# A Fourier mixing layer and its channel mix: sequence split 24x128 to 48x64, feature butterfly, paired planes, mirrored half by exchanged weight rows, squares on DVE alone

## Chip, cores and metric

One Trainium2 chip, one core. The metric is the device time of one execution in microseconds. The kernel before has three measured runs: 703.01, 699.72 and 702.3 us, median 702.3.

## The reference, cut to what matters

```python
def reference(x, mu_k, mu_r, w_k, w_v, w_r):      # x: 8 x 3072 x 256
    y = np.fft.fft(np.fft.fft(x, axis=1), axis=2).real
    y_prev = np.concatenate([zeros(8, 1, 256), y[:, :-1, :]], axis=1)
    xk = mu_k * y + (1 - mu_k) * y_prev
    xr = mu_r * y + (1 - mu_r) * y_prev
    k = np.maximum(xk @ w_k, 0)                    # 256 -> 1024
    v = (k * k) @ w_v                              # 1024 -> 256
    r = 1 / (1 + np.exp(-(xr @ w_r)))
    return r * v                                   # 8 x 3072 x 256, f32
```

The input of the channel mix is real, so the half of the spectrum past row 1536 is that of the mirrored row with the feature index mirrored as well: y[S-k, v] = y[k, (256-v) mod 256].

## The kernel before

Each of the 8 batches goes through two parts. The **Fourier part** writes the sequence index as n1 x 128 with n1 = 24. Stage A (`stage_a_group`, L240) multiplies 64 blocks of the loaded `xh` (96 partitions) by a 104-wide table and gives `a_sb`; ACT and DVE take turns at moving its PSUM tile to SBUF (L250, L252). Stage D (`dc_d_step`, L297 to L304) is the Fourier transform over the 256 features: for each of 13 values of k1 two or four matmuls of 512 columns into `psG`, which DVE casts to `g_sb` (L307). Stage C (`dc_c_step`, L313, L316) is the remaining transform over 128, in four 128-wide matmuls, moved by ACT (L319). `refl_step` (L329 to L335) makes the 11 mirrored slabs of y with four matmuls each by two reflection matrices, moved by ACT (L337).

The **channel mix** works in 6 chunks of 512 sequence positions. `mix_block` (L266 to L269) forms xk and xr on DVE. `moe_kmm` runs 8 feature groups per chunk: two 512-wide matmuls into `psK` (L388, L391), a Relu on ACT over 512 columns (L394), and a square (L397) on POOL for even and on DVE for odd groups. `moe_vr` runs, for each of four blocks of 128 positions, eight 256-wide matmuls with w_v (L407) and two with w_r (L412) into one PSUM tile; ACT takes the Sigmoid (L416), DVE multiplies (L418) and SP stores 128 KB (L420).

`stage_moe` sets the order: the kmm block of a chunk (16 matmuls), then two or three `dc_steps` of the next batch with stage A groups of the batch after it, then the vr block of the chunk before. Loads of x are issued by POOL (L221), between its squares. PSUM has six one-bank buffers for everything but `psKV`, which has two. The tables (wd, cm, sm) are made in a prologue on DVE and ACT.

Of the kernel before, what the change touches and what calls it, by code (L numbers as in the profile page):

```python
# [23 lines left out]

@with_exitstack
def kernel(
# [10 lines left out]
    nc = tc.nc  # L39
# [27 lines left out]
    nc.vector.tensor_scalar(out=pcol_f, in0=pcol_i, scalar1=1.0, scalar2=None,
                            op0=ALU.mult)

    col256_i = gen.tile([P, 256], INT32)  # L70
    nc.gpsimd.iota(col256_i, pattern=[[1, 256]], base=0, channel_multiplier=0)
    col128_i = gen.tile([P, 128], INT32)
    nc.gpsimd.iota(col128_i, pattern=[[1, 128]], base=0, channel_multiplier=0)
    col24_i = gen.tile([P, 24], INT32)
    nc.gpsimd.iota(col24_i, pattern=[[1, 24]], base=0, channel_multiplier=0)

    def gen_trig(dst_cos, dst_sin, p_vals, col_i, scale, ncols, pn,
                 sin_scale=1.0, dst_nsin=None):
        u = gen.tile([P, 256], FP32, name="gen_u")[:pn, :ncols]
        r = gen.tile([P, 256], FP32, name="gen_r")[:pn, :ncols]  # L80
        ci = col_i[:pn, :ncols]
        nc.vector.tensor_scalar(out=u, in0=ci, scalar1=p_vals, scalar2=scale,
                                op0=ALU.mult, op1=ALU.mult)
        nc.vector.tensor_scalar(out=r, in0=u, scalar1=MAGIC, scalar2=MAGIC,
                                op0=ALU.add, op1=ALU.subtract)
        nc.vector.tensor_tensor(out=u, in0=u, in1=r, op=ALU.subtract)
        if dst_sin is not None:
            nc.scalar.activation(out=dst_sin, in_=u, func=AF.Sin,
                                 bias=0.0, scale=TWO_PI * sin_scale)
        if dst_nsin is not None:  # L90
            nc.scalar.activation(out=dst_nsin, in_=u, func=AF.Sin,
                                 bias=0.0, scale=-TWO_PI)
        nc.vector.tensor_scalar(out=u, in0=ci, scalar1=p_vals, scalar2=scale,
                                op0=ALU.mult, op1=ALU.mult)
        nc.vector.tensor_scalar(out=u, in0=u, scalar1=0.25, scalar2=None,
                                op0=ALU.add)
        nc.vector.tensor_scalar(out=r, in0=u, scalar1=MAGIC, scalar2=MAGIC,  # L97
                                op0=ALU.add, op1=ALU.subtract)
        nc.vector.tensor_tensor(out=u, in0=u, in1=r, op=ALU.subtract)
        nc.scalar.activation(out=dst_cos, in_=u, func=AF.Sin, bias=0.0,  # L100
                             scale=TWO_PI)

    NKH = 13
    w24_mov = const.tile([96, 4, NKH, 2], FP16)
    nc.vector.memset(w24_mov, 0.0)
    w24_blk = gen.tile([24, NKH, 2], FP16)
    col13_i = gen.tile([P, NKH], INT32)
    nc.gpsimd.iota(col13_i, pattern=[[1, NKH]], base=0, channel_multiplier=0)
    gen_trig(dst_cos=w24_blk[:, :, 0], dst_sin=w24_blk[:, :, 1],
             p_vals=pcol_f[:24], col_i=col13_i, scale=1.0 / N1, ncols=NKH, pn=24,  # L110
             sin_scale=-1.0)
    for g in range(4):
        nc.sync.dma_start(out=w24_mov[24 * g:24 * g + 24, g], in_=w24_blk[:, :, :])
    refl_corner = const.tile([P, 128], FP16)
    refl_anti = const.tile([P, 128], FP16)
    nc.gpsimd.memset(refl_corner, 0.0)
    nc.gpsimd.affine_select(out=refl_corner, in_=refl_corner,
                            compare_op=ALU.not_equal, fill=1.0, base=0,
                            pattern=[[1, 128]], channel_multiplier=1)
    nc.gpsimd.memset(refl_anti, 0.0)  # L120
    nc.gpsimd.affine_select(out=refl_anti, in_=refl_anti,
                            compare_op=ALU.not_equal, fill=1.0, base=-128,
                            pattern=[[1, 128]], channel_multiplier=1)

    wd_r = [const.tile([P, 512], FP16, name=f"wd_r{da}") for da in range(2)]
    wd_i = [const.tile([P, 512], FP16, name=f"wd_i{da}") for da in range(2)]
    dval = gen.tile([P, 1], FP32)
    for da in range(2):
        nc.vector.tensor_scalar(out=dval, in0=pcol_f, scalar1=1.0,
                                scalar2=float(128 * da), op0=ALU.mult, op1=ALU.add)  # L130
        u = gen.tile([P, 256], FP32, name="gen_u")
        r = gen.tile([P, 256], FP32, name="gen_r")
        nc.vector.tensor_scalar(out=u, in0=col256_i, scalar1=dval, scalar2=1.0 / D,
                                op0=ALU.mult, op1=ALU.mult)
        nc.vector.tensor_scalar(out=r, in0=u, scalar1=MAGIC, scalar2=MAGIC,
                                op0=ALU.add, op1=ALU.subtract)
        nc.vector.tensor_tensor(out=u, in0=u, in1=r, op=ALU.subtract)
        nc.scalar.activation(out=wd_i[da][:, 0:256], in_=u, func=AF.Sin,
                             bias=0.0, scale=TWO_PI)
        nc.scalar.activation(out=wd_r[da][:, 256:512], in_=u, func=AF.Sin,  # L140
                             bias=0.0, scale=-TWO_PI)
        nc.vector.tensor_scalar(out=u, in0=u, scalar1=0.25, scalar2=None,
                                op0=ALU.add)
        nc.vector.tensor_scalar(out=r, in0=u, scalar1=MAGIC, scalar2=MAGIC,
                                op0=ALU.add, op1=ALU.subtract)
        nc.vector.tensor_tensor(out=u, in0=u, in1=r, op=ALU.subtract)
        nc.scalar.activation(out=wd_r[da][:, 0:256], in_=u, func=AF.Sin,
                             bias=0.0, scale=TWO_PI)
        nc.scalar.activation(out=wd_i[da][:, 256:512], in_=u, func=AF.Sin,
                             bias=0.0, scale=TWO_PI)  # L150
# [12 lines left out]
    tmp_m = gen.tile([P, 128], FP32)
    for k1 in range(13):
        cb = cosb[:, k1:k1 + 1]
        sb = sinb[:, k1:k1 + 1]
        nsb = nsinb[:, k1:k1 + 1]
        nc.scalar.activation(out=tmp_m, in_=c128, func=AF.Copy, scale=cb)
        nc.vector.scalar_tensor_tensor(out=cm_all[:, k1], in0=s128, scalar=nsb,
                                       in1=tmp_m, op0=ALU.mult, op1=ALU.add)  # L170
        tmp_m2 = gen.tile([P, 128], FP32, name="tmp_m2")
        nc.scalar.activation(out=tmp_m2, in_=s128, func=AF.Copy, scale=cb)
        nc.vector.scalar_tensor_tensor(out=sm_all[:, k1], in0=c128, scalar=sb,
                                       in1=tmp_m2, op0=ALU.mult, op1=ALU.add)
# [10 lines left out]
    def load_weights():  # L185
# [3 lines left out]
        for fc in range(8):  # L189
            nc.gpsimd.dma_start(out=wv_sb[:, fc], in_=wv_dram[fc])  # L190
# [319 lines left out]
```

## Time and profile before

| what | value |
|---|---|
| three runs | 699.72 to 703.01 us, median 702.3 us |
| span of the profiled execution | 697.3 us (its own time is given by this span; the median lies 5.0 us above it) |
| PE busy | 567.6 us, 81% |
| DVE busy | 562.8 us, 81% |
| ACT busy | 380.9 us, 55% |
| POOL busy | 266.0 us, 38% |
| moved by DMA | 39.7 MB, mean 57 GB/s |

Busy shares are averages over the span. Matmuls overlap each other, so PE's busy time counts more than the time between their starts, and the starts tell the rate.

### The profile page before, as it was taken

Reading aid. Unit: us, or ns where it says so; the run is one execution under the profiler, and the core shown is the slowest. Engines: PE = TensorE matmul, PEld = TensorE weight load, DVE = VectorE, ACT = ScalarE, POOL = GpSimd, SP = SyncE. Lnnn points to the kernel's source line nnn. Section 1 sums busy time; section 2 is a strip of 40 time slices with the busy share of each in tenths; the row PEclk is TensorE's granted clock in tenths of the full one; section 3 lists DMA queues with packets and bytes.
Section 4 is the critical chain, followed back from the end, with each engine's and each line's share of the span. In section 5 each row is a group of like instructions: output and inputs, shape, how many; then the busy total and the mean of one; then the engine's idle time right before and its main releaser. Section 6 shows DMA issues by size and latency. Waiting matters only on the chain.

```text
span 697.3 us, 11974 instructions
## 1 busy us (share of the span) xinstructions
PE 567.6 (81%) x4352; PEld 390.1 (56%) x4352; DVE 562.8 (81%) x1036; ACT 380.9 (55%) x955; POOL 266.0 (38%) x281
## 2 busy tenths in 40 slices
PE   0297689887988798887898889989797988988897
PEld 0265366564656556664566546656565645656565
DVE  4569988698797968988887888879889797869764
ACT  3855456545565465554554565565565554555564
POOL 6323333424253243234422353252343253342552
PEclk9999799999999999999999999999999999999999
DMA  6740131042111430032301422111010110111112
GB/s 120 130 91 13 29 83 62 30 106 47 54 39 39 110 65 31 31 86 62 66 31 47 91 48 60 46 45 63 23 39 31 46 47 31 54 39 62 46 60 78
DMA packets 33227, 39.72 MB, mean 57 GB/s; under 512 B 5520, under 2 KB 31376, under 8 KB 31632
## 3 DMA queue, kind: packets, MB, share of 16 engines
q0 software_dynamic: 4800, 13.77, 11.5%
q1 hardware_dynamic: 28368, 25.19, 10.8%
q8 instruction: 34, 0.56, 0.4%
q14 instruction: 25, 0.20, 0.1%
HBM read 27.53 MB, written 25.17 MB: 76 GB/s over the span
## 4 chain that ended last, share of the span: by engine, by line
DVE 54%; PE 23%; ACT 12%; issue 6%; DMA 4%; SPq 0%; ACTq 0%; DVEq 0%
DVE k2t L397 21%; PE psKV L407 12%; ACT k2t L394 9%; DVE xr_sb L267 9%; DVE g_sb L307 6%; DVE xk_sb L269 6%; DVE xk_sb L266 4%; DMA out_dram<-o_sb 3%; DVE o_sb L418 3%; PE psKV L412 3%; DVE a_sb L252 2%; PE psK L388 2%; PE psK L391 2%; PE psY L313 1%; ACT a_sb L250 1%
## 5 line engine op out<-in xcount | busy, mean ns | idle before, releaser
L397 POOL TENSOR_TENSOR k2t<-k2t 128x512 f16<-128x512 f16 x192 | 225.7, 1202 | 392.0 <-ACT k2t L394 391.8
L407 PE MATMUL psKV<-wv_sb,k2t 128*128 128x256 f16 x1536 | 206.5, 277 | 17.9 <-DVE o_sb L418 16.0
L397 DVE TENSOR_TENSOR k2t<-k2t 128x512 f16<-128x512 f16 x192 | 186.5, 999 | 31.3 <-ACT k2t L394 28.4
L394 ACT ACTIVATE k2t<-psK 128x512 f16<-128x512 f32 x384 | 195.0, 627 | 15.8 <-PE psK L391 11.7
L407 PEld LDWEIGHTS <-k2t 128*128 128x128 f16 x1536 | 150.4, 99 | 48.5 <-issue 26.5
L416 ACT ACTIVATE r_sb<-psKV 128x256 f16<-128x256 f32 x192 | 73.6, 383 | 160.9 <-PE psKV L412 159.5
L388 PE MATMUL psK<-xk_sb,wk_sb 128*128 128x512 f16 x384 | 149.9, 390 | 5.2 <-DVE a_sb L252 4.6
L391 PE MATMUL psK<-xk_sb,wk_sb 128*128 128x512 f16 x384 | 149.7, 390 | 0.0
L418 DVE TENSOR_TENSOR o_sb<-psKV,r_sb 128x256 f32<-128x256 f32 x192 | 79.8, 418 | 75.4 <-ACT r_sb L416 67.6
L319 ACT ACTIVATE y_sb<-psY 128x256 f16<-128x256 f32 x104 | 40.0, 385 | 120.6 <-PE psY L316 119.9
L313 PE MATMUL psY<-cm_all,g_sb 128*128 128x128 f16 x208 | 35.4, 224 | 71.3 <-DVE g_sb L307 71.0
L269 DVE SCALAR_TENSOR_TENSOR xk_sb<-xk_sb,mu_k,y_sb 128x512 f16<-128x512 f16 (+2 forms) x112 | 85.7, 769 | 0.2
L267 DVE SCALAR_TENSOR_TENSOR xr_sb<-xk_sb,mu_r,y_sb 128x512 f16<-128x512 f16 (+2 forms) x112 | 84.4, 763 | 0.0
L307 DVE CAST g_sb<-psG 128x512 f16<-128x512 f32 x104 | 70.3, 677 | 11.1 <-PE psG L299 7.9
L412 PE MATMUL psKV<-wr_sb,xr_sb 128*128 128x256 f16 x384 | 74.3, 276 | 0.0
L313 PEld LDWEIGHTS <-g_sb 128*128 128x128 f16 x208 | 19.2, 98 | 97.4 <-DVE g_sb L307 92.5
L240 PE MATMUL psA<-w_mov,xh 96*128 96x104 f16 x512 | 44.8, 221 | 29.2 <-DVE gen_r L97 16.6
L391 PEld LDWEIGHTS <-wk_sb 128*128 128x128 f16 x384 | 38.3, 100 | 48.0 <-issue 10.1
L388 PEld LDWEIGHTS <-wk_sb 128*128 128x128 f16 x384 | 38.6, 101 | 40.9 <-issue 5.0
L240 PEld LDWEIGHTS <-xh 96*128 96x128 f16 x512 | 33.8, 103 | 32.2 <-DMA xh<-in_x_dram 16.6
L250 ACT ACTIVATE a_sb<-psA 128x208 f16<-128x208 f32 x144 | 45.3, 397 | 0.9 <-PE psA L240 0.9
L297 PE MATMUL psG<-wd_r,a_sb 128*128 128x512 f16 x104 | 41.0, 394 | 1.9 <-DVE g_sb L307 1.9
(76 smaller groups left out, 570.0 us busy)
## 6 DMA issues: line engine op xcount, KB each, us to landing
out_dram<-o_sb SPq DMA_DIRECT2D x192, 128.0 KB, 1.7
xh<-in_x_dram POOLq DMA_DIRECT2D x64, 192.0 KB, 4.6
wk_sb<-in_moe_w_k_dram POOLq DMA_DIRECT2D x2, 256.0 KB, 10.0
wv_sb<-in_moe_w_v_dram POOLq DMA_DIRECT2D x8, 64.0 KB, 5.5
wr_sb<-in_moe_w_r_dram POOLq DMA_DIRECT2D x2, 64.0 KB, 2.4
w_mov<-w_blk SPq DMA_DIRECT2D x4, 1.2 KB
mu_k<-in_moe_mu_k_dram SPq DMA_DIRECT2D x2, 0.5 KB, 2.0
mu_r<-in_moe_mu_r_dram SPq DMA_DIRECT2D x2, 0.5 KB, 2.2
```

The costliest lines, as they stand in the source:

```text
L240: nc.tensor.matmul(out=pa[:, jj * 104:(jj + 1) * 104], lhsT=xh[:, j * 128:(j + 1) * 128], rhs=w24_mov[:, :, :, :], start=True, stop=True,)
L267: nc.vector.scalar_tensor_tensor(out=dr, in0=dk, scalar=mu_r_sb[vh], in1=prv, op0=ALU.mult, op1=ALU.add)
L269: nc.vector.scalar_tensor_tensor(out=dk, in0=dk, scalar=mu_k_sb[vh], in1=prv, op0=ALU.mult, op1=ALU.add)
L307: nc.vector.tensor_copy(out=g_sb, in_=gp)
L388: nc.tensor.matmul(out=kp, lhsT=wk_sb[0][:, fc * 128:(fc + 1) * 128], rhs=xk_flat[0][:, tch * 512:(tch + 1) * 512], start=True, stop=False)
L391: nc.tensor.matmul(out=kp, lhsT=wk_sb[1][:, fc * 128:(fc + 1) * 128], rhs=xk_flat[1][:, tch * 512:(tch + 1) * 512], start=False, stop=True)
L394: nc.scalar.activation(out=k2t[:, 0, fc], in_=kp, func=AF.Relu, bias=0.0, scale=0.25)
L397: sq_eng.tensor_tensor(out=k2t[:, 1, fc], in0=k2t[:, 0, fc], in1=k2t[:, 0, fc], op=ALU.mult)
L407: nc.tensor.matmul(out=kvp[:, 0:256], lhsT=k2t[:, 1, fc, tb * 128:(tb + 1) * 128], rhs=wv_sb[:, fc], start=(fc == 0), stop=(fc == 7))
L412: nc.tensor.matmul(out=kvp[:, 256:512], lhsT=xr_flat[vh][:, k1 * 128:(k1 + 1) * 128], rhs=wr_sb[vh], start=(vh == 0), stop=(vh == 1))
L416: nc.scalar.activation(out=r_sb, in_=kvp[:, 256:512], func=AF.Sigmoid)
L418: nc.vector.tensor_tensor(out=o_sb, in0=kvp[:, 0:256], in1=r_sb, op=ALU.mult)
```

## The change

The sequence index is written as 48 x 64, and only 25 of the 48 values of k1 (27 slabs with neighbours) are computed.

- `butterfly` (DVE): x is split into the sum and the difference of its two feature halves, 96 partitions x 16 x 128 each, two instructions per half batch.
- `a_item` (16 per batch): four 96-wide matmuls for four sequence rows; `d_item` (12): four 128-wide matmuls for two values of k1, in place of eight 512-wide ones; `c_item` (7): three matmuls (128, 128, 64 wide) for each of up to four slabs.
- `refl_step` is gone. The mirrored chunks use the same slabs, reversed in time by the write of `mix` (L377), and weights whose rows are exchanged (`wk[1]`, `wr[1]`, made once).
- `mix` works per pair of chunks: one subtraction, then products with mu by `tensor_scalar` and additions.
- In `k_half` one PSUM tile holds two feature groups: one Relu over 1024 columns, and one square over 2048 columns for four groups, always on DVE. `r_pair` and `v_tile`: Sigmoid, product and PSUM tile are 512 wide.
- Past the first batch, all evacuations of the Fourier part are on ACT (`evac`). POOL issues loads only.
- PSUM: two buffers of two banks for K, two of one bank for V, and two of one bank (`psF`) shared by A, D, C and R.
- The order is a loop of 24 steps per batch: two K groups, an item of the next batch's Fourier part between and behind them, and one V tile of the chunk five steps back.

```diff
-            sq_eng = nc.gpsimd if fc % 2 == 0 else nc.vector
-            sq_eng.tensor_tensor(out=k2t[:, 1, fc], in0=k2t[:, 0, fc],
-                                 in1=k2t[:, 0, fc], op=ALU.mult)
...
+    def ps_f(name):
+        return psum.tile([P, 512], FP32, name=name, tag="psF", bufs=2)
...
+    def butterfly(b, h):
+        xh = xh_t.pop((b, h))
+        eo = eo_pool.tile([96, 16, 2, 128], FP16, name="eo")
+        V.tensor_tensor(out=eo[:, :, 0], in0=xh[:, :, 0:128], in1=xh[:, :, 128:256],
+                        op=ALU.add)
+        V.tensor_tensor(out=eo[:, :, 1], in0=xh[:, :, 0:128], in1=xh[:, :, 128:256],
+                        op=ALU.subtract)
...
+    def evac(out_ap, in_ap, both):
+        evac_n[0] += 1
+        if both and evac_n[0] % 2:
+            V.tensor_copy(out=out_ap, in_=in_ap)
+        else:
+            nc.scalar.activation(out=out_ap, in_=in_ap, func=AF.Copy)
...
+        for i in range(4):                                   # a_item
+            nc.tensor.matmul(out=ps[:, 96 * i:96 * i + 96],
+                             lhsT=eo[:, 4 * grp + i, e, :], rhs=w_a[0:96],
+                             start=True, stop=True)
+        src = _v(ps, 0, [(2, 48), (96, 4), (1, 2)])
+        dst = _v(a_t[b][e], 8 * (4 * h + grp), [(64, 48), (2, 4), (1, 2)])
+        evac(dst, src, both)
...
+        for i in range(2):                                   # d_item
+            u = 2 * up + i
+            for e in range(2):
+                nc.tensor.matmul(out=_v(ps, 256 * i + 64 * (1 - e), [(128, 2), (1, 64)]),
+                                 lhsT=a_t[b][e][:, 2 * u:2 * u + 2, :],
+                                 rhs=w_eo[:, e, :], start=True, stop=True)
+        evac(g_of(2 * up)[:, :, 1:257], ps.rearrange("p (i c) -> p i c", i=2), both)
...
+        for a in range(2):                                   # k_half
+            nc.tensor.matmul(out=st["kp"][:, 512 * hs:512 * hs + 512],
+                             lhsT=wk_sb[m][a][:, 128 * fc:128 * fc + 128],
+                             rhs=xk[:, a, m], start=(a == 0), stop=(a == 1))
+        if hs == 1:
+            nc.scalar.activation(out=st["rl"][:, 2 * ds:2 * ds + 2],
+                                 in_=st["kp"].rearrange("p (f t) -> p f t", f=2),
+                                 func=AF.Relu, bias=0.0, scale=0.25)
+            if ds % 2:
+                r = st["rl"][:, 2 * ds - 2:2 * ds + 2]
+                V.tensor_tensor(out=k2_t[c][:, 2 * ds - 2:2 * ds + 2], in0=r, in1=r,
+                                op=ALU.mult)
...
+    for step in range(nk + LAG):                             # LAG = 5, nk = 192
+        q, b = step % 24, step // 24
+        if step < nk:
+            c, ds = chunks[step // 4], step % 4
+            k_half(c, ds, 0, kst)
+            due(q)
+            k_half(c, ds, 1, kst)
+        vs = step - LAG
+        if vs >= 0:
+            cv, tb = chunks[vs // 4], vs % 4
+            if tb % 2 == 0:
+                r_pair(cv, tb // 2, vst)
+            v_tile(cv, tb, vst)
+        due(q + 0.5)
+        if q in (20, 21) and b + 2 < B:
+            butterfly(b + 2, q - 20)
+        if q in (3, 11) and b < B:
+            mix(b, 1 if q == 3 else 2)
+        if q == 20 and b + 1 < B:
+            mix(b + 1, 0)
```

A scheduler places the instructions of each engine, so their order is not quite that of the loop. Three places follow, as the built programs have them. `psF` tiles are named by their use (psA, psD, psC, psR).

First, ACT in the middle of the program. Before, between two chunks of a steady batch:

```order
L416 ACTIVATE r_sb<-psKV 128x256 [waits DVE_49,PE_49] x8
L394 ACTIVATE k2t<-psK 128x512 [waits PE_49,Pool_49]
L394 ACTIVATE k2t<-psK 128x512 [waits PE_49] x7
L319 ACTIVATE y_sb<-psY 128x2x128 [waits PE_49]
L394 ACTIVATE k2t<-psK 128x512 [waits PE_49,Pool_49]
```

And of the change, in the part of a batch in which D and C items run:

```order
L416 ACTIVATE r<-psR 128x512 [waits DVE_49,PE_49]
L288 ACTIVATE g_173<-psD 128x2x256 [waits PE_49,Pool_49]
L398 ACTIVATE rl<-psK 128x1024 [waits PE_49]
L288 ACTIVATE g_170<-psD 128x2x256 [waits PE_49,Activation_49]
L288 ACTIVATE y<-psC 128x2x256 [waits PE_49]
L398 ACTIVATE rl<-psK 128x1024 [waits PE_49]
```

Runs of eight Relus have become single wide ones with evacuations of D and C between them, and no ACT instruction of the steady part waits for a square on POOL (the one Pool wait here is for the first clearing of a `g` buffer).

Second, DVE in a steady batch. Before, around a run of squares:

```order
L269 SCALAR_TENSOR_TENSOR xk_sb<-xk_sb,mu_k_257,y_sb 128x512 [waits DVE_49]
L397 TENSOR_TENSOR k2t<-k2t 128x512 [waits Activation_49,Pool_49]
L267 SCALAR_TENSOR_TENSOR xr_sb<-xk_sb,mu_r_260,y_sb 128x512
L397 TENSOR_TENSOR k2t<-k2t 128x512 [waits Activation_49]
L269 SCALAR_TENSOR_TENSOR xk_sb<-xk_sb,mu_k_258,y_sb 128x512 [waits DVE_49]
```

And of the change:

```order
L403 TENSOR_TENSOR k_1464<-rl 128x2048 [waits Activation_49]
L430 TENSOR_TENSOR o<-psV,r 128x512 [waits DMAHW2_49,DMAHW3_49,PE_49,Activation_49]
L375 TENSOR_TENSOR x_1723<-t,y 128x2x512 [waits PE_49]
L377 TENSOR_TENSOR x_1723<-t,y 128x2x512
L403 TENSOR_TENSOR k_1464<-rl 128x2048 [waits Activation_49]
L430 TENSOR_TENSOR o<-psV,r 128x512 [waits DMAHW4_49,DMAHW5_49,PE_49,Activation_49]
```

The parts of a `mix` stand between squares and products and not in one block, and the squares are four times as wide.

Third, the start of DVE's stream. Before:

```order
L105 MEMSET w_mov 96x52
L201 TENSOR_SCALAR om_k_261<-mu_k_257 128x1 [waits DMAHW0_49]
L204 TENSOR_SCALAR om_r_263<-mu_r_259 128x1 [waits DMAHW1_49]
L201 TENSOR_SCALAR om_k_262<-mu_k_258 128x1 [waits DMAHW2_49]
L204 TENSOR_SCALAR om_r_264<-mu_r_260 128x1 [waits DMAHW3_49]
L67 TENSOR_SCALAR pcol_f<-pcol_i 128x1 [waits Pool_49]
```

And of the change:

```order
L265 TENSOR_SCALAR mum_191<-muf_189 128x1 [waits DMAHW6_49,DMAHW5_49,DMAHW4_49]
L144 TENSOR_TENSOR eo<-xh 96x16x128 [waits DMASW1_49,DMASW0_49]
L146 TENSOR_TENSOR eo<-xh 96x16x128
L144 TENSOR_TENSOR eo<-xh 96x16x128 [waits DMASW3_49,DMASW2_49]
L146 TENSOR_TENSOR eo<-xh 96x16x128
L106 CAST pcol_f<-pcol_i 128x1 [waits Pool_49]
```

The first batch's four butterflies, which wait for the loads of x (DMASW), now stand ahead of `pcol_f`, from which every table is made.

## Rows read from the trace of the kernel before

**Rows 1.** The page's head and part 1: busy us (share of span) xinstructions

```profile
span 697.3 us, 11974 instructions
...
PE 567.6 (81%) x4352; PEld 390.1 (56%) x4352; DVE 562.8 (81%) x1036; ACT 380.9 (55%) x955; POOL 266.0 (38%) x281
```

**Rows 2.** Busy time by stretch: PE, PEld, DVE, ACT, POOL, clock, DMA

```profile
150.00:230.00 80.00, 68.45 (x533) 46.80 (x533) 67.07 (x122) 44.36 (x110) 31.64 (x32) 0.98 0.22 57
```

**Rows 3.** The chain that ended last, by engine and line

```profile
DVE k2t L397 21%; PE psKV L407 12%; ACT k2t L394 9%; DVE xr_sb L267 9%; DVE g_sb L307 6%; DVE xk_sb L269 6%; DVE xk_sb L266 4%; DMA out_dram<-o_sb 3%; DVE o_sb L418 3%; PE psKV L412 3%; DVE a_sb L252 2%; PE psK L388 2%; PE psK L391 2%; PE psY L313 1%; ACT a_sb L250 1%
```

**Rows 4.** Timeline of DVE, 236 to 270 us: start us, us, engine line, operation

```profile
240.56 1.38 DVE L397 TENSOR_TENSOR k2t<-k2t 128x512 f16<-128x512 f16 x1
...
242.52 0.41 DVE L397 TENSOR_TENSOR k2t<-k2t 128x512 f16<-128x512 f16 x1
242.86 0.68 DVE L307 CAST g_sb<-psG 128x512 f16<-128x512 f32 x1
```

**Rows 5.** Timeline of POOL in the same stretch

```profile
240.59 1.05 POOL L397 TENSOR_TENSOR k2t<-k2t 128x512 f16<-128x512 f16 x1
```

**Rows 6.** Timeline of PE, 236 to 262 us

```profile
238.08 0.38 PE L388 MATMUL psK<-xk_sb,wk_sb 128*128 128x512 f16 x1
238.30 0.38 PE L391 MATMUL psK<-xk_sb,wk_sb 128*128 128x512 f16 x1
...
243.59 0.23 PE L313 MATMUL psY<-cm_all,g_sb 128*128 128x128 f16 x1 [3.23 <-DVE g_sb L307]
...
243.77 0.22 PE L316 MATMUL psY<-sm_all,g_sb 128*128 128x128 f16 x1
...
250.10 0.22 PE L313 MATMUL psY<-cm_all,g_sb 128*128 128x128 f16 x1
...
250.32 0.44 PE L240 MATMUL psA<-w_mov,xh 96*128 96x104 f16 x6
250.60 0.40 PE L297 MATMUL psG<-wd_r,a_sb 128*128 128x512 f16 x1
...
254.33 1.04 PE L407 MATMUL psKV<-wv_sb,k2t 128*128 128x256 f16 x8
255.20 0.38 PE L412 MATMUL psKV<-wr_sb,xr_sb 128*128 128x256 f16 x2
```

**Rows 7.** Timeline of ACT: runs of one kind at 641, at 30, and one evacuation

```profile
641.29 6.96 ACT L394 ACTIVATE k2t<-psK 128x512 f16<-128x512 f32 x14
...
29.87 7.64 ACT L250 ACTIVATE a_sb<-psA 128x208 f16<-128x208 f32 x32
...
244.03 0.38 ACT L319 ACTIVATE y_sb<-psY 128x256 f16<-128x256 f32 x1 [3.77 <-PE psY L316]
```

**Rows 8.** Groups by form: line engine op, out<-in, xcount | busy us, mean ns | idle

```profile
L316 PEld LDWEIGHTS <-g_sb 128*128 128x128 f16 x208 | 20.6, 99 | 6.0 <-issue 0.7
...
L282 DVE TENSOR_SCALAR xk_sb<-y_sb,mu_k 128x1 f16<-128x1 f16 x16 | 3.2, 202 | 0.0
...
L191 DVE TENSOR_SCALAR wv_sb<-wv_sb 128x2048 f16<-128x2048 f16 x1 | 0.7, 685 | 0.0
...
L100 ACT ACTIVATE w_blk<-gen_u 24x13 f16<-24x13 f32 x1 | 0.2, 223 | 1.0 <-DVE gen_u L99 1.0
...
L88 ACT ACTIVATE sinb<-gen_u 128x24 f32<-128x24 f32 x1 | 0.2, 223 | 0.7 <-DVE gen_u L86 0.7
```

**Rows 9.** Timeline of DVE, 647 to 655 us, and the last DVE instruction of the program

```profile
651.49 0.74 DVE L418 TENSOR_TENSOR o_sb<-psKV,r_sb 128x256 f32<-128x256 f32 x2
...
694.27 0.42 DVE L418 TENSOR_TENSOR o_sb<-psKV,r_sb 128x256 f32<-128x256 f32 x1 [0.67 <-ACT r_sb L416]
```

**Rows 10.** Timeline of the prologue: loads of x on POOL, and PE's first K matmul

```profile
2.48 4.79 POOL L221 DMA_DIRECT2D xh<-in_x_dram  x9
...
15.31 0.50 POOL L221 DMA_DIRECT2D xh<-in_x_dram  x1 [0.76 <-DMA xh<-in_x_dram]
...
59.84 0.38 PE L388 MATMUL psK<-xk_sb,wk_sb 128*128 128x512 f16 x1
```

More of the change, by code (lines that the diff above doesn't have):

```diff
@@ L75 @@
[L75 to L113, printed above, removed]
@@ L125 @@
[L125 to L150, printed above, removed]
@@ L163 @@
[L163 to L174, printed above, removed]
@@ new lines, in ps_v, with load_xh @@
+    def ps_v():
+        return psum.tile([P, 512], FP32, name="psV", tag="psV", bufs=2)
+    def ps_f(name):
+        return psum.tile([P, 512], FP32, name=name, tag="psF", bufs=2)
+    x_r = x.rearrange("b (n1 r) d -> b n1 r d", r=R)
+    xh_t = {}
+    eo_t = {}
+    def load_xh(b, h):
+        xh = xh_pool.tile([96, 16, 256], FP16, name="xh")
+        for g in range(2):
+            nc.gpsimd.dma_start(
+                out=xh[48 * g:48 * g + 48],
+                in_=x_r[b, :, 32 * g + 16 * h:32 * g + 16 * h + 16, :])
+        xh_t[b, h] = xh
@@ new lines, in permute_weights @@
+    def permute_weights():
+        V.tensor_copy(out=perm_f, in_=perm)
+        for h in range(2):
+            ps = ps_v()
+            nc.tensor.matmul(out=ps, lhsT=perm, rhs=wk_hi[:, 512 * h:512 * h + 512],
+                             start=True, stop=True)
+            V.tensor_copy(out=wk_sb[0][1][:, 512 * h:512 * h + 512], in_=ps)
+        ps = ps_v()
+        nc.tensor.matmul(out=ps[:, 0:256], lhsT=perm, rhs=wr_hi, start=True, stop=True)
+        V.tensor_copy(out=wr_sb[0][1], in_=ps[:, 0:256])
+        ps = ps_v()
+        nc.tensor.matmul(out=ps[:, 0:2], lhsT=perm_f, rhs=mu_hi, start=True, stop=True)
+        for i in range(2):
+            V.tensor_copy(out=mu_f[i][:, 1:2], in_=ps[:, i:i + 1])
@@ new lines, in g_of, with d_item @@
+    def g_of(u):
+        return g_t[0] if u < 2 else g_t[1 + (u // 2 - 1) % (NG - 1)]
+    def d_item(b, up, both=False):
+        ps = ps_f("psD")
+        for i in range(2):
+            u = 2 * up + i
[4 more added lines that the diff above has]
+        evac(g_of(2 * up)[:, :, 1:257], ps.rearrange("p (i c) -> p i c", i=2), both)
@@ new lines, in c_item @@
+    def c_item(b, grp, both=False):
+        if grp == 0:
+            y_t[b] = y_pool.tile([P, 2, NSL, 64], FP16, name="y")
+        ps = ps_f("psC")
+        n = min(4, NSL - 4 * grp)
+        for i in range(n):
+            sl = 4 * grp + i
+            k1 = sl - 1
+            u = {-1: 1, 24: 0, 25: 23}.get(k1, k1)
+            g = g_of(u)[:, u % 2]
+            o = ps[:, 128 * i:128 * i + 128]
+            nc.tensor.matmul(out=o, lhsT=g[:, 128:256],
+                             rhs=_v(m1, 64 * sl, [(0, 2), (1, 64)]), start=True, stop=False)
+            nc.tensor.matmul(out=o, lhsT=g[:, 0:128], rhs=m2[:, sl], start=False, stop=False)
+            nc.tensor.matmul(out=o[:, 64:128], lhsT=g[:, 256:384], rhs=m1[:, sl],
+                             start=False, stop=True)
+        src = _v(ps, 0, [(64, 2), (128, n), (1, 64)])
+        evac(y_t[b][:, :, 4 * grp:4 * grp + n, :], src, both)
@@ new lines, in dft_items @@
+    def dft_items(b, both=False):
+        items = []
+        for h in range(2):
+            for grp in range(4):
+                for e in range(2):
+                    items.append(lambda h=h, grp=grp, e=e: a_item(b, h, grp, e, both))
+        na = len(items)
+        done = -1
+        for grp in range(7):
+            need = min(4 * grp + 2, 23) if grp < 6 else 23
+            while 2 * done + 1 < need:
+                done += 1
+                items.append(lambda up=done: d_item(b, up, both))
+            items.append(lambda grp=grp: c_item(b, grp, both))
+        return items, na
@@ new lines, in r_pair @@
+    def r_pair(c, tp, st):
+        b, i, m = c
+        ps = ps_f("psR")
+        for h in range(2):
+            tb = 2 * tp + h
+            for a in range(2):
+                nc.tensor.matmul(out=ps[:, 256 * h:256 * h + 256],
+                                 lhsT=x_t[b, i][1][:, a, m, 128 * tb:128 * tb + 128],
+                                 rhs=wr_sb[m][a], start=(a == 0), stop=(a == 1))
+        st["r"] = o_pool.tile([P, 512], FP16, name="r")
+        nc.scalar.activation(out=st["r"], in_=ps, func=AF.Sigmoid)
@@ new lines, in v_tile @@
+    def v_tile(c, tb, st):
+        b, i, m = c
+        h = tb % 2
+        if h == 0:
+            st["v"] = ps_v()
+        for fc in range(8):
+            nc.tensor.matmul(out=st["v"][:, 256 * h:256 * h + 256],
+                             lhsT=k2_t[c][:, fc, 128 * tb:128 * tb + 128],
+                             rhs=wv_sb[:, fc], start=(fc == 0), stop=(fc == 7))
+        if h == 0:
+            return
+        o = o_pool.tile([P, 2, 256], FP32, name="o")
+        V.tensor_tensor(out=o.rearrange("p a b -> p (a b)"), in0=st["v"], in1=st["r"],
+                        op=ALU.mult)
+        for s in range(2):
+            if m == 0:
+                k = 8 * i + 2 * (tb - 1) + s
+            else:
+                k = 40 - 8 * i + 2 * (tb - 1) + s
+            dst = dataclasses.replace(out[b, k:k + 1, :], ap=[[48 * D, 64], [2 * D, 2], [1, D]])
+            nc.sync.dma_start(out=dst, in_=o[64 * s:64 * s + 64])
@@ new lines, with due @@
+    load_xh(1, 1)
+    items0, _ = dft_items(0, both=True)
+    for it in items0:
+        it()
+    permute_weights()
+    derive_weights()
+    mix(0, 0)
+    butterfly(1, 0)
+    butterfly(1, 1)
+    chunks = [(b, i, m) for b in range(B) for i in range(3) for m in range(2)]
+    LAG = 5
+    nk = 4 * len(chunks)
+    pend = []
+    kst, vst = {}, {}
+    def due(t):
+        while pend and pend[0][0] <= t:
+            pend.pop(0)[1]()
+    for step in range(nk + LAG):
+        q, b = step % 24, step // 24
+        if q == 0 and b + 1 < B:
+            items, na = dft_items(b + 1)
+            rest = items[na:]
+            pend = [(10.0 * n / na, it) for n, it in enumerate(items[:na])]
+            pend += [(10.0 + 11.0 * n / len(rest), it) for n, it in enumerate(rest)]
+        if step < nk:
[10 more added lines that the diff above has]
+        due(q + 0.5)
+        if q in (0, 2) and b + 2 < B:
+            load_xh(b + 2, q // 2)
+        if q in (20, 21) and b + 2 < B:
[4 more added lines that the diff above has]
+            mix(b + 1, 0)
```

507 lines of the change are left out of this document (193 added, 314 removed).

## The prediction

> **What bounds the kernel now.** I read the head of the page first [rows 1]: PE and DVE are both busy for 81% of the span, and POOL, with 38%, is not far from idle. The stretch from 150 to 230 us [rows 2] shows that this is the steady state: in 80 us PE is busy for 68.5 and DVE for 67.1, at a granted clock of 0.98, so the clock is not what is short. The chain that ended last [rows 3] names the one that decides: the square on DVE (L397) has 21% of it, more than any matmul, and the mix and cast lines on DVE follow. The timeline then shows why those squares are dear. A square takes 1.38 us when POOL runs its own square in the same moment [rows 4, 5], and 0.41 us when POOL is silent, the next instruction starting 0.34 us behind it [rows 4]. PE pays for this: a C matmul waited 3.23 us for DVE's cast [rows 6], and the K and V work stood queued behind it.
>
> PE's own need can be counted from starts. Two 512-wide matmuls start 0.22 us apart; eight 256-wide ones take 0.87 us, 0.109 each (so 0.216 for 512); four 128-wide ones take 0.22 us, 0.055 each; six 104-wide ones 0.28 us, 0.047 each [rows 6]. A batch has 96 K (20.7 us), 192 V (20.9), 48 R (5.2), 48 D of 512 (10.4), 96 C and reflection matmuls of 128 (5.3) and 64 A (3.0): 65.5 us. From the first K matmul at 59.8 us [rows 10] to the end of the span is 637.5 us, or 79.7 per batch. So 14.2 us per batch are waits, most of them behind DVE. A change gains by PE columns only if DVE is relieved too. This one does both.
>
> **The change, part by part.** *PE.* K, V and R stay (46.8 us). A stays at 64 matmuls, at most 3.0 us. D becomes 48 matmuls of 128 in place of 512: 2.6 us, 7.8 less. C becomes 54 of 128 and 27 of 64; a 64-wide one costs between 0.027 (half of 0.055) and 0.055, and I take the latter, since each also loads 128 columns of weights: 4.5 us, 0.8 less. Sum 56.9 us per batch, 8.6 less.
>
> *DVE.* The order of the change has no square on POOL, so I price 16-bit two-input work at the undisturbed 0.34 us for 512 [rows 4]: 12 squares of 2,048 at 1.36 (16.3 us), four butterflies at 1.36 (5.4), and in each of three mixes one subtraction (0.85 or 0.68) and four additions of 1,024 at 0.68 (10.3 together). The 24 products with mu are one-input work on 512: between 0.20, which one column takes, and 0.69, which 2,048 take [rows 8]; a quarter of the way is 0.32 (7.7 us). Twelve output products of 512 cost at most twice the 0.37 of the 256-wide pair [rows 9]: 8.9 us. Sum 48.6 us of DVE per batch, against 67 in each 80 before. It was the bound and now has slack.
>
> *ACT.* Fourteen Relus of 512 take 6.96 us, 0.50 each, and 32 evacuations of 208 take 7.64, 0.24 each [rows 7]; between them lie 0.85 ns per column. So 24 Relus of 1,024 cost 0.93 each (22.3 us), 12 Sigmoids of 512 0.50 (6.0), 16 A evacuations of 384 0.39 (6.2), 12 of D 0.50 (6.0) and seven of C 3.4: 44 us per batch. The A evacuation writes pairs of elements far apart; the trace has one write of single elements two apart, 13 of them in 223 ns, as long as 24 contiguous ones [rows 8], so I add nothing, and at worst a doubling of 6.2 us, which still leaves ACT under PE. ACT becomes the second engine, at 44 of about 60 us. [...]
>
> *POOL and SP.* POOL keeps the loads alone, in the same bytes; they are issued most of a batch before their butterfly, against under 13 us for all of the first batch [rows 10]. SP still issues 24 stores of 128 KB per batch. I cost both at nothing, covered by that slack.
>
> *What is late next.* Where the wait for DVE goes, PE next meets the evacuations on ACT: A, D, C and R share two PSUM buffers. From the last C matmul's start to its free buffer is 0.22 + 0.04 + 0.38 us at 256 columns [rows 6, 7], so about 0.85 for 512. Mostly 0.9 to 1.7 us of K, R and V work lie between two uses. Only where a C item follows its D by two K matmuls (0.43 us), three or four times a batch, does PE lose some 0.45: 2 us. A square or product late behind a mix costs perhaps another 1.5. I take 3.5 us of waits per batch; the bounds are 1 (all hidden) and 9 (two thirds of what is there now).
>
> *Prologue and end.* Before, K starts at 59.8 us. In the change the four loads of the first batch carry what eight carried, which had landed at about 15.3 us after a first issue at 2.5 [rows 10]; issued some 1.5 us earlier, they land by about 14, and the butterflies, which now stand first on DVE, hold the tables back until about 16. Then DVE has some 85 instructions before the first K can start: three butterflies (4), 19 casts at 0.6 to 0.7 (12), six passes of 1,728 f32 columns at 1 to 2 us (9), weight copies (5), half a mix (4), and some 40 small ones at 0.2 (8), about 42. So K starts near 57; bounds 50 and 65. At the end, as before, a product, and 2.6 us from the last DVE instruction [rows 9] to the end of the span: 3.5.
>
> *The sum.* 57 + 7 batches of 56.9 with Fourier work (398) + the last without (46.8) + waits (7 times 3.5, and 1) + 3.5 = 531 us of span. The profiled execution has 697.3, its median 702.3; I carry the 5.0 over: **536 us**.
>
> **The rivals.**
> - *The scheduler's order does not fit, and PE waits as much as now* (14.2 us per batch): 536 + 7 x 10.7 + 4 = 615. For it: the stream of every engine is strict, and ACT and DVE each have one queue for Fourier and mix work. Against it: no engine but PE needs more than about 80% of the batch's time.
> - *DVE's wide instructions run slower than the silent 0.34*, at one column per 1.2 ns or so (0.6 for 512), because of their strides or reversed writes: squares 29, butterflies 10, mixes 18 + 8, products 9, 74 us per batch, so DVE is the bound: 57 + 7 x 74 + 52 + 4 + 5 = 636. Against it: the square at 242.52 [rows 4] needs no special pattern, and only the reversed addition does. With that one alone slow (6 us more), nothing changes.
> - *Small matmuls go at the pace of their weight loads.* A weight load is 99 ns long [rows 8]. If each of the 193 small matmuls took that, a batch would gain 9 us: 536 + 63 = 599. Against it: every such matmul loads its weights (208 loads for L316 [rows 8]), and the four at 250.10 took 55 ns each all the same [rows 6]. The Trainium skill (TensorE: Matmul & The Clock Gate, section Back-to-back issue gap) gives about 81 ns for a 128-wide matmul in a stream with weight loads; by that estimate the time would be near 575. The trace's 55 ns disagrees.
> - *Slower than before: the two shared buffers.* If PE stood through the 0.85 us round trip at each of the 47 items of A, D, C and R in a batch, that is 40 us per batch and about 790 in all. It decides from 32 of the 47 on: 7 x 32 x 0.85 = 190 us on top of 511, which is the sum with the 5.0 and without waits, makes 701. Against it: the order puts K or V matmuls between nearly all of them.
>
> **How the numbers follow.** My forecast, PE as the bound with short waits, has 0.80. The order that does not fit has 0.08, slow DVE 0.05, the weight loads 0.04, the shared buffers 0.03. My own case reaches from 512 (prologue 50, waits of 1) to 591 (prologue 65, waits of 9). The range that should hold 8 in 10 is **513 to 600**; it takes in the weight loads and leaves out the other three rivals (0.16) and what lies under its low end. Faster by over 0.5%, which is about what three runs of this kernel can tell from no change, takes all cases but the last: 0.96; the same 0.01; slower 0.03.
>
> **What would show it.** Right: squares of 2,048 on DVE at or under 1.4 us; PE the engine with the longest chain share and no wait behind DVE over 2 us in the steady part; about 60 us between the first K matmuls of two batches; ACT near 75% busy; the first K near 57 us. Wrong: a square near 2.2 us or more, PE waits on ACT that sum to over 10 us per batch, 128-wide matmuls 0.08 or more apart, or a first K behind 65 us.

## The result and the profile after

The changed kernel takes **507.0 us** (median of four runs, 505.1 to 508.4); the kernel before, run beside it, 701.0. The ratio is 0.722 with a 95% interval of 0.719 to 0.725. The forecast was 536 with a range of 513 to 600: right in sign and cause, but 29 us too long, with the measured time below the range. The profiled execution took 508.4 us, 1.8 more than its span.

The head, part 1 and the chain of the page after (the counterpart of [rows 1, 3]):

```profile
span 506.6 us, 10507 instructions
...
PE 466.0 (92%) x4237; PEld 345.7 (68%) x4237; DVE 368.2 (73%) x618; ACT 380.5 (75%) x557; POOL 31.2 (6%) x58
...
PE 88%; DMA 3%; ACT 3%; POOL 3%; DVE 2%; issue 1%; POOLq 0%; DVEq 0%; ACTq 0%
```

The chain is PE's now, where DVE had the largest share. Two stretches of 57 us (columns: us, then busy time of PE, PEld, DVE, ACT, POOL, then clock, DMA share, GB/s), against [rows 2]:

```profile
114.00:171.00 57.00, 57.00 (x536) 42.53 (x535) 42.73 (x68) 48.43 (x73) 2.06 (x4) 1.00 0.39 85
171.00:228.00 57.00, 57.00 (x537) 42.64 (x535) 42.58 (x67) 48.42 (x72) 2.05 (x4) 1.00 0.38 84
```

PE is never idle in them, DVE fell from 67 busy in 80 us to 43 in 57. And PE waited once, from the first K matmul to the end (the view of PE's waits: us in total, times, longest):

```profile
PE psK L394 <- ACT rl L398: 0.3, 1, 0.3
```

Before, the same view of the stretch from 60 us on begins with

```profile
PE psY L313 <- DVE g_sb L307: 70.4, 42, 4.1
PE psKV L407 <- DVE o_sb L418: 16.0, 22, 2.0
```

The last three batches begin 56.4 us apart (PE's timeline after, the rows of their first K matmuls):

```profile
336.75 0.59 PE L394 MATMUL psK<-x,wk 128*128 128x512 f16 x2
...
393.14 0.59 PE L394 MATMUL psK<-x,wk 128*128 128x512 f16 x2
...
449.54 1.03 PE L394 MATMUL psK<-x,wk 128*128 128x512 f16 x4
```

So the time went where it was looked for: by the prediction's count (first K matmul to the end of the span, over eight batches) 79.7 us a batch became 56.2, and the waits are gone. Which part of the change took which share, the runs tell.

### The profile page after: what moved, and what is told of

It reads as the page before. It is cut to its first block, busy times and chain, and to the rows that moved or that the text cites. A ratio compares the mean times of both kernels' runs of the same rounds, so it can differ in the third digit from the quotient of the medians.

```text
span 506.6 us, 10507 instructions
## 1 busy us (share of the span) xinstructions
PE 466.0 (92%) x4237; PEld 345.7 (68%) x4237; DVE 368.2 (73%) x618; ACT 380.5 (75%) x557; POOL 31.2 (6%) x58
## 4 chain that ended last, share of the span: by engine, by line
PE 88%; DMA 3%; ACT 3%; POOL 3%; DVE 2%; issue 1%; POOLq 0%; DVEq 0%; ACTq 0%
PE psV L424 33%; PE psK L394 32%; PE psR L412 8%; PE psD L311 5%; PE psA L296 4%; PE psC L327 3%; PE psC L329 3%; DMA xh<-in_x_dram 2%; PE psC L330 1%; DMA rl<-in_moe_w_k_dram 1%; ACT rl L398 1%; ACT a L288 1%; POOL xh L82 1%; POOL g L208 1%; POOL perm L242 0%
## 5 line engine op out<-in xcount | busy, mean ns | idle before, releaser
L398 ACT ACTIVATE rl<-psK 128x1024 f16<-128x1024 f32 x192 | 196.7, 1024 | 35.2 <-PE psK L394 35.2
L394 PE MATMUL psK<-x,wk 128*128 128x512 f16 x768 | 219.3, 380 | 0.5 <-ACT rl L398 0.3
L424 PE MATMUL psV<-wv_sb,k 128*128 128x256 f16 x1536 | 198.7, 273 | 0.0
L424 PEld LDWEIGHTS <-k 128*128 128x128 f16 x1536 | 150.1, 98 | 36.8
L403 DVE TENSOR_TENSOR k<-rl 128x2048 f16<-128x2048 f16 x96 | 117.3, 1222 | 41.5 <-ACT rl L398 40.6
L430 DVE TENSOR_TENSOR o<-psV,r 128x512 f32<-128x512 f32 x96 | 66.0, 687 | 51.6 <-PE psV L424 34.5
L394 PEld LDWEIGHTS <-wk 128*128 128x128 f16 x768 | 62.7, 98 | 19.4 <-issue 1.1
L288 ACT ACTIVATE a<-psA 128x384 f16<-128x384 f32 x120 | 58.6, 497 | 18.0 <-PE psA L296 14.1
L412 PE MATMUL psR<-wr,x 128*128 128x256 f16 x384 | 57.6, 272 | 0.1
L327 PE MATMUL psC<-m,g 128*128 128x128 f16 x216 | 38.9, 229 | 1.1 <-ACT g L288 0.8
L329 PE MATMUL psC<-m,g 128*128 128x128 f16 x216 | 39.1, 230 | 0.0
```

Of the source, the lines that this page charges most:

```text
L288: nc.scalar.activation(out=out_ap, in_=in_ap, func=AF.Copy)
L327: nc.tensor.matmul(out=o, lhsT=g[:, 128:256], rhs=_v(m1, 64 * sl, [(0, 2), (1, 64)]), start=True, stop=False)
L329: nc.tensor.matmul(out=o, lhsT=g[:, 0:128], rhs=m2[:, sl], start=False, stop=False)
L394: nc.tensor.matmul(out=st["kp"][:, 512 * hs:512 * hs + 512], lhsT=wk_sb[m][a][:, 128 * fc:128 * fc + 128], rhs=xk[:, a, m], start=(a == 0) ...
L398: nc.scalar.activation(out=st["rl"][:, 2 * ds:2 * ds + 2], in_=st["kp"].rearrange("p (f t) -> p f t", f=2), func=AF.Relu, bias=0.0, scale= ...
L403: V.tensor_tensor(out=k2_t[c][:, 2 * ds - 2:2 * ds + 2], in0=r, in1=r, op=ALU.mult)
```

## The experiments

### How much were the squares on POOL? (two kernels made from the one before)

```diff
-            sq_eng = nc.gpsimd if fc % 2 == 0 else nc.vector
+            sq_eng = nc.vector
```

> The kernel before with all its squares on DVE, none on POOL. Contention theory (POOL's squares stretch DVE's from 0.41 to 1.38 us, and that is what PE waits for): DVE squares fall to 0.4 us or less, the waits of 14.2 us a batch fall to 5 or less, time near 625 us (610 to 650). Order theory (the waits come from the coarse blocks, 16 K matmuls and then whole Fourier steps, whatever engine squares): squares get faster too, but the time stays at 680 or more. Load theory (DVE has simply too much work): 192 more squares on DVE make it the bound, time 690 or more with DVE over 90% busy.

Measured: **623.0 us** (ratio 0.888, 0.885 to 0.892). This one line gives 79 of the 195 us (the kernel before ran at 702.3 beside this one). DVE now does all 384 squares. The page's groups (count, busy us, mean ns, idle before), first of the kernel before, then of this run:

```profile
L397 DVE TENSOR_TENSOR k2t<-k2t 128x512 f16<-128x512 f16 x192 | 186.5, 999 | 31.3 <-ACT k2t L394 28.4
```
```profile
L397 DVE TENSOR_TENSOR k2t<-k2t 128x512 f16<-128x512 f16 x384 | 155.1, 421 | 19.7 <-ACT k2t L394 7.5
```

192 squares more cost DVE less time than before: 155 us here, where it needed 186.5 for half as many, 999 ns each. Of PE's waits behind the cast 4.4 us are left of 70.4 (PE's waits in this run):

```profile
PE psKV L407 <- DVE o_sb L418: 21.4, 15, 4.7
PE psY L313 <- DVE g_sb L307: 4.4, 18, 0.4
```

The second kernel also moved the stage D casts and all A evacuations to ACT:

```diff
-        nc.vector.tensor_copy(out=g_sb, in_=gp)
+        nc.scalar.activation(out=g_sb, in_=gp, func=AF.Copy)
...
-        if b == 0 or grp % 2 == 0:
+        if True:
```

> The same, and the casts of stage D and all evacuations of stage A on ACT as well, so that DVE has some 15 us a batch less and ACT some 10 more. Contention theory: nothing much on top of the run without POOL, within 15 us of it. Load theory: the large gain comes only here, time near 600 us. Order theory: 650 us or more all the same.

Measured: 621.0 us, 2 less (intervals 0.885 to 0.892 and 0.882 to 0.886 overlap). The load theory falls: once POOL is out of the way, DVE's work is covered also in the old order. The order theory had 680 or more and 650 or more for the two kernels; it falls as well.

### What held the old order at 623?

The wait that is left is behind the product. Products and loads in that run (DVE's and POOL's timelines):

```profile
208.57 0.42 DVE L418 TENSOR_TENSOR o_sb<-psKV,r_sb 128x256 f32<-128x256 f32 x1 [3.85 <-DMA out_dram<-o_sb]
```
```profile
197.96 3.93 POOL L221 DMA_DIRECT2D xh<-in_x_dram  x8 [72.30 <-PE psA L240]
```

With no square between them, POOL issues the eight loads of a batch within 4 us (before, they were spread over some 28 us, 224.1 to 252.2 for one batch); the stores beside them land late (10.7 us at most, median 1.7), and the product has no output tile to write. PE stands, and its clock goes with it (stretches, columns as above):

```profile
205.00:209.00 4.00, 0.35 (x3) 0.07 (x1) 0.43 (x2) 0.38 (x1) 0.00 (x0) 0.91 0.75 157
209.00:213.00 4.00, 3.34 (x16) 2.15 (x16) 2.18 (x5) 0.38 (x1) 0.00 (x0) 0.50 0.61 168
```

```diff
-            o_sb = small.tile([P, 256], FP32, name="o_sb")
+            o_sb = small.tile([P, 256], FP32, name="o_sb", bufs=9)
```

> The kernel before with all squares on DVE and nine buffers in place of four for the output tile (and for the gate, from the same pool: that one stays at four). Store theory (what is left of PE's waits there, 21.4 us behind the product, comes from eight products that waited 23.7 us in all for a store that landed late): those waits go, near 600 us (595 to 607). Rival (something else holds PE right after): 615 us or more.

Measured: **593.0 us** (0.845, 0.843 to 0.847), 30 less, somewhat more than the 21.4 of waits: the mean granted clock went from 0.978 to 1.000 as well. Its batches are 68.6 us long (two of them begin at 403.8 and 472.4), against PE's 65.5: the old order leaves 3.1 us of waits a batch when neither POOL nor the stores disturb it.

### Squares on POOL in the new order

```diff
-                V.tensor_tensor(out=k2_t[c][:, 2 * ds - 2:2 * ds + 2], in0=r, in1=r,
+                sq = nc.gpsimd if ds == 1 else V
+                sq.tensor_tensor(out=k2_t[c][:, 2 * ds - 2:2 * ds + 2], in0=r, in1=r,
```

> The changed kernel with every second square of 2048 on POOL (6 of 12 a batch). Contention theory: POOL needs near 5 us for each, 29 us a batch; beside it DVE's two-input work takes up to three times as long, DVE loses some 20 us a batch and stands over 57 us, PE waits return: 550 to 620 us. Rival (DVE has 14 us of slack a batch and V comes five steps behind K, so it is covered): 505 to 515 us.

Measured: 517.8 us (0.737, 0.735 to 0.739). Neither: 11 us more, of which 9.1 are one wait, of the first V matmuls for a square on POOL. The obstruction is there in full, in both directions. Timelines of DVE, POOL and PE:

```profile
200.14 4.37 DVE L144 TENSOR_TENSOR eo<-xh 96x2048 f16<-96x2048 f16 x1 [1.61 <-PE psA L296]
```
```profile
199.83 3.60 POOL L404 TENSOR_TENSOR k<-rl 128x2048 f16<-128x2048 f16 x1 [3.17 <-ACT rl L398]
...
59.48 11.86 POOL L404 TENSOR_TENSOR k<-rl 128x2048 f16<-128x2048 f16 x1 [12.15 <-ACT rl L398]
```
```profile
71.40 0.61 PE L425 MATMUL psV<-wv_sb,k 128*128 128x256 f16 x2 [9.07 <-POOL k L404]
```

Against DVE: the butterfly, 1.22 us by itself, ends 1.08 us after POOL's square does: it was not slowed, it stood until POOL had finished. Read the same way, the 1.38 us of [rows 4, 5] are some 1.0 of standing beside POOL's square of 1.05, and the undisturbed 0.34; that is a reading, since the record of DVE's square there begins 0.03 us ahead of POOL's. Against POOL: the square at 59.48 found DVE at work on mixes without a gap until 67.9, and took its 3.5 us only then; for that one PE waited 9.07. In the steady part the new order covers both. The Trainium skill (SBUF — State Buffer, section Who interferes with whom) says that VectorE and GpSimd share a pair of ports under an exclusive lock, held for a whole instruction; the trace agrees. A product that reads PSUM went through beside POOL's square of 209.97 to 213.57 in its usual 0.69 us.

### Are PE's columns the time?

Each stage D matmul is issued four times into the same place:

```diff
+                for _ in range(4):
                     nc.tensor.matmul(out=_v(ps, 256 * i + 64 * (1 - e), [(128, 2), (1, 64)]),
```

> The changed kernel with each of the 48 matmuls of stage D issued four times into the same place, so that stage D has the 24,576 columns a batch that it had before. Column theory (PE is the bound with almost no waits, each 128-wide matmul costs 0.055 us): 144 more a batch, 7.9 us, 55 us over seven batches and some 3 to 8 in the prologue: 566 us (558 to 575). Weight-load rival (0.08 us for each): 590 us. Slack rival (PE still has waits that take up part of it): under 545 us.

Measured: **566.5 us** (0.807, 0.805 to 0.809), as forecast for PE as a strict bound. The first K matmul is at 56.7 us, where it was at 56.8, so all of it falls behind the prologue: 58.8 us of span over 7 x 144 matmuls are 0.058 us each, although each of them loads its weights again (the run has 1,536 weight loads for 1,536 stage D matmuls). The Trainium skill (TensorE: Matmul & The Clock Gate, section Back-to-back issue gap) has 81 ns for such a stream, which, as an estimate, would have made 82 us; the measurement decides against it here.

### Why are there no waits? Three attempts on the order's slack

One PSUM buffer for A, D, C and R; items handed out every fourth step; V four steps behind K:

```diff
-        return psum.tile([P, 512], FP32, name=name, tag="psF", bufs=2)
+        return psum.tile([P, 512], FP32, name=name, tag="psF", bufs=1)
```

> The changed kernel with one PSUM buffer in place of two for A, D, C and R. Round-trip theory (47 uses a batch, each needs its buffer for 0.85 us and more; some half of them follow the one before with only a K pair or less between, 0.43 us): 24 times 0.4 us, near 10 us of PE waits a batch, 575 us (540 to 640). Rival (the scheduler sets V matmuls between, so the round trip stays covered): 505 to 520 us.

Measured: 565.2 us (0.806, 0.804 to 0.808), in the range of the round-trip theory. Its profiled span is 56 us longer; 10.5 of them are in the prologue (first K at 67.3), the rest is 6.5 us a batch.

```diff
-            due(q)
             k_half(c, ds, 1, kst)
...
-        due(q + 0.5)
+        if q % 4 == 3:
+            due(q + 0.5)
```

> The changed kernel with its Fourier items handed out every fourth step in groups instead of one by one. If the fine interleaving is what removes the waits: groups of four to six items, each with 0.3 to 0.5 us of its round trip uncovered, some 10 us a batch, 560 to 600 us. If the slack of DVE and ACT alone does it: 505 to 520 us.

Measured: 526.8 us (0.751, 0.749 to 0.754), between the two: some 3 us a batch. The scheduler drew K and V matmuls between the grouped items again, so this says little of really coarse blocks.

```diff
-    LAG = 5
+    LAG = 4
```

> The changed kernel with V four steps behind K in place of five. If the distance of V is what covers late squares: V of a chunk stands one K pair behind the last square's Relu (1.02 and 1.22 us, and what is ahead of them in both queues), some 1.5 us of wait for each of 48 chunks, 530 to 575 us. If the scheduler and the slack of DVE and ACT cover it: 503 to 510 us.

Measured: 510.7 us (0.728, 0.725 to 0.730), a little over the rival's numbers and far under the other's. PE's weight loads for V waited 4.2 us in all for squares, at most 0.6 each.

So the second buffer is needed, the fine interleaving is worth some 3 us a batch, and the fifth step is hardly needed. That the slack of DVE and ACT covers the rest is the explanation that is left; no run shows it by itself.

### Evacuations on DVE

```diff
-        if both and evac_n[0] % 2:
+        if not both or evac_n[0] % 2:
```

> The changed kernel with the evacuations of A, D and C of all batches but the first on DVE in place of ACT. By the rows (0.55 to 0.69 us each on DVE, DVE busy 42.6 of 57 us): 22 us more for DVE, 64 a batch, so DVE becomes the bound: 565 us (545 to 590). [...]

Measured: 531.8 us (0.758, 0.757 to 0.759). DVE becomes the bound, by less than forecast: a batch takes 59.8 us and not 64, since one DVE instruction begins some 0.08 us before the one ahead of it ends, and the forecast added whole durations of the casts. A stretch of this run (columns as above), and two groups of DVE's instructions (busy us, mean ns, idle before):

```profile
114.00:171.00 57.00, 55.79 (x509) 39.69 (x508) 56.75 (x95) 29.52 (x34) 2.06 (x4) 1.00 0.32 72
```
```profile
L286 DVE CAST a<-psA 128x384 f16<-128x384 f32 x120 | 63.1, 547 | 1.8 <-PE psA L296 1.7
L286 DVE CAST g<-psD 128x512 f16<-128x512 f32 x90 | 60.0, 687 | 3.6 <-PE psD L311 3.4
```

In the changed kernel ACT moves the same tiles in 497 and 602 ns, so for these sums out of PSUM ACT is the faster of the two.

### The prologue

In the change two of DVE's first instructions, products with -1, wait for the loads of mu, 256 bytes each, which land 5.4 and 10.7 us after their issue beside the loads of x; butterflies and tables stand behind them (DVE's timeline):

```profile
7.89 0.15 DVE L265 TENSOR_SCALAR mum<-muf 128x1 f32<-128x1 f32 x1 [6.84 <-DMA muf<-in_moe_mu_k_dram]
15.16 0.15 DVE L265 TENSOR_SCALAR mum<-muf 128x1 f32<-128x1 f32 x1 [7.11 <-DMA muf<-in_moe_mu_r_dram]
15.26 1.22 DVE L144 TENSOR_TENSOR eo<-xh 96x2048 f16<-96x2048 f16 x1
```

Three kernels go on from there, each from the one ahead of it. The first and the third make several edits at once, so that their gain is that of the edits together.

```diff
-    load_xh(0, 0)
-    load_xh(0, 1)
...
+    load_xh(0, 0)
     nc.gpsimd.iota(kcol_i, pattern=[[1, NSL], [48, 64]], base=-1, channel_multiplier=0)
+    load_xh(0, 1)
...
-            load_lo(nc.sync, mu_f[i][:, 0:1], mu2)
+            load_lo(nc.gpsimd, mu_f[i][:, 0:1], mu2)
```

(mu_hi likewise, and the butterflies behind the tables.)

> The changed kernel with the prologue put in another order: iotas first, the eight tiny mu loads behind the weights on POOL's queue, table passes ahead of the butterflies on DVE. If DVE's wait for the mu loads (14.4 us idle before 15.3) and the tables behind it set the first K at 56.8 us: first A matmul near 16 us instead of 25.6, first K near 47, time near 497 us (493 to 502). If the landing of x or the evacuations of the first batch set it: first K still 53 or later, 503 to 508 us.

Measured: 499.4 us (0.712, 0.710 to 0.714); the first A matmul at 12.8 us, the first K at 48.0.

```diff
+        if b == 0 and pf_n[0] % 4 in (1, 2):
+            return psum.tile([P, 1024], FP32, name=name, tag="psK", bufs=2)[:, 0:512]
```

> The same, and two more PSUM buffers (those of K, idle until then) for A, D and C of the first batch. If PE waits for buffers there (0.3 to 0.8 us per item, 35 items): first K another 5 us earlier, 492 us. If the evacuations by DVE and ACT set the pace (35 of 0.5 to 0.7 us and DVE's other work): within 2 us of the run before it.

Measured: 498.9 us, first K at 47.0: no difference that the times can tell. But its timelines of DVE and POOL show another thing (third, the same pass in the kernel that follows, where POOL has no memset):

```profile
4.70 4.29 DVE L112 TENSOR_SCALAR reo<-ueo 128x256 f32<-128x256 f32 x1
```
```profile
5.36 3.47 POOL L211 MEMSET g<- 128x768 f16 x5
```
```profile
5.28 0.29 DVE L112 TENSOR_SCALAR reo<-ueo 128x256 f32<-128x256 f32 x1
```

A pass of 0.29 us took 4.29 and ended 0.16 us after POOL's memsets did: the same kind of obstruction, now beside work that only writes on POOL's side. The record of the pass begins 0.66 us before the memsets, and what held it in that time is not shown.

```diff
-        nc.gpsimd.memset(gt, 0.0)
+        V.memset(gt[:, :, 0:1], 0.0)
+        V.memset(gt[:, :, 257:GU], 0.0)
...
-    for it in items0:
+    for it in items0[:16]:
         it()
     permute_weights()
     derive_weights()
+    for it in items0[16:25]:
+        it()
     mix(0, 0)
+    for it in items0[25:]:
+        it()
+    derive_mirror()
```

(perm is zeroed on DVE too, the casts of the exchanged weights go to ACT, and `derive_mirror` is a part of `derive_weights` that now comes later.)

> The prologue of the run with tables first and two more PSUM buffers, and: the zeroing of g on DVE in place of POOL (in that run one DVE pass of 256 columns took 4.29 us beside POOL's memsets), the weight casts on ACT, the first mix right behind the third C item, the second batch's butterflies behind it. If DVE's chain of work sets the first K (42 of the first 48 us busy): first K near 40 us in place of 47.0, time near 491.5 us (488 to 495). If the landing of x and of the weights sets it: first K 45 or later, 497 us or more.

Measured: **493.7 us** (0.703, 0.702 to 0.705). It is faster than both kernels, 13 us faster than the changed one, which stands at 0.722 (0.719 to 0.725). K matmuls by tile (count, min/median/max ns, first and last start):

```profile
L399 PE MATMUL psK<-x,wk x768: 376/379/634, 42.5 to 480.6; 128*128 128x512 f16 x192
```

The first K came 4.5 us earlier than in the run before it, of the 7 expected; it falls between the two cases of the expectation, and what holds it there is open.

## Why the prediction was right, and where it was off

The bound and the cause were right, the number was not: two terms of the sum, the waits of the batches and the 5.0 us carried over, were together some 29 us too large.

*The bound.* Right. PE's need without waits, 7 x 56.9 + 46.8 = 445.1 us, is what passed: the first K matmul starts at 56.8, and the last V matmuls end at 501.9. Two small errors cancel in that: a steady batch took 56.4 us and not 56.9, and some 3.6 us more than was counted passed outside the steady batches. The small matmuls cost what [rows 6] said, and the run with fourfold stage D makes it a strict bound. The 64-wide matmuls, taken at 0.055, cost about 0.03 (202.53 to 202.56 below), some 0.7 us less a batch.

*The waits, 3.5 us a batch: this step failed.* It put 25.5 us into the sum. From the first K matmul on, 0.3 came on PE itself, and some 4.5 in short waits of its weight loads, which overlap the matmuls; a steady batch is no longer than its columns alone were taken to be. The argument let C stand until its D's cast had ended. But a C item works through four slabs (its first six items do, the seventh has three), and only the fourth reads that D. In PE's and ACT's timelines after:

```profile
201.76 0.39 PE L311 MATMUL psD<-w_eo,a 128*128 128x128 f16 x4
201.99 0.59 PE L394 MATMUL psK<-x,wk 128*128 128x512 f16 x2
202.42 0.22 PE L327 MATMUL psC<-m,g 128*128 128x128 f16 x1
...
202.53 0.19 PE L330 MATMUL psC<-m,g 128*128 128x64 f16 x1
202.56 0.22 PE L327 MATMUL psC<-m,g 128*128 128x128 f16 x1
...
202.90 0.23 PE L327 MATMUL psC<-m,g 128*128 128x128 f16 x1
```
```profile
202.25 0.60 ACT L288 ACTIVATE g<-psD 128x512 f16<-128x512 f32 x1
```

C starts in its turn at 202.42; the cast ends at 202.85, and the fourth slab starts at 202.90, about 0.06 late. The prediction counted 0.45 for that place. The 1.5 us for late squares and products did not come either; the run with V a step closer shows that they had a step to spare. Its lower bound of 1 a batch was not low enough.

*The 5.0 us carried over: the second term that failed, by 3.2 us.* It set the median of three runs against the span of a fourth execution; what lies outside the span is 1.8 us in this profiled run and 1.7 to 2.2 in the other kernels here. With the end, which was 1.2 us too short, the two terms make up the difference between 536 and the profiled 508.4.

*DVE.* Right: squares of 2,048 at 1.22 us (1.36 taken), additions at 0.69 (0.68), the reversed one 0.68, no penalty; 43 of 57 us busy (48.6 a batch taken). That they were dear beside POOL was right too, but it is no slowing: they stand in line.

*ACT.* 48.4 of 57 us, taken 44: Relus of 1,024 at 1.02 (0.93), A at 0.497 (0.39), D and Sigmoid at 0.60 (0.50). It stayed the second engine.

*Prologue and end.* First K forecast near 57, measured 56.8, partly by luck: the small loads of mu were not seen as the thing that holds DVE. The end took 4.7 us from the last V matmul (3.5 taken).

*The waits of the kernel before* were counted too low. The 79.7 us are a mean over eight batches, of which the last has no Fourier work, while the need of 65.5 includes it. The first K matmul of the first batch starts at 59.84 [rows 10], that of the last batch at 632.15 (PE's timeline before). So the seven batches between took 81.8 us each, and some 16 of those were waits, not 14.2. The forecast counts up from PE's need and does not rest on it; the rival of an order that does not fit would have stood near 630.

*The rivals.* None came. The rival of weight loads is refuted by 0.058 us each, the order that does not fit by 0.3 us of waits. The shared buffers were far off: even one buffer in place of two costs 6.5 us a batch and not 40, as K and V matmuls lie between most uses. Wide instructions run at the pace of narrow ones: 1.22 us for a square of 2,048, four times 0.34 for 512.

*Shares of the 195 us,* by the chain of kernels: squares off POOL 79, stores no longer waited for 30, and 86 for the rest of the change. Of those, as an estimate, 8.6 us of columns over seven batches make 60, the 3.1 us of remaining waits 22, the earlier first K 3; no run takes these apart. The first two could be had in the old order.

## What to carry to other kernels

Before an engine's long instructions are called its own cost, look at what its neighbour does in the same moment: the squares given to an idle POOL cost DVE more than they saved it (DVE was busy with squares for 186.5 us when it had half of them, and for 155.1 when it had all), and in the old order PE paid for it. Price a wait at the instruction that really reads the late tile, not at the first of its group. And after a bound is removed, look for transfers that now bunch up.

## What was not expected of the hardware

- Beside loads that POOL issued in one go (eight within 3.9 us), stores landed after up to 10.7 us where 1.7 is usual; PE, having stood 3.7 us, then ran at a granted clock of 0.50 for the next 4 us, its lower level.
- DVE holds POOL up as POOL does DVE: a square of 3.6 us took 11.86 while DVE worked without a gap. A DVE pass of 0.29 us took 4.29 beside POOL's memsets, though they read nothing.
- A load of 256 bytes took 10.7 us to land beside 1.5 MB of x.
